# The second layer's up products by Strassen's scheme, over pairs of chunks

## The chip, the cores and the metric

The kernel runs on one core of one Trainium2 chip. The metric is the device time of one execution, in microseconds, as the median of several runs. Beside it there is one profiled execution, whose trace gives every instruction's start and duration on each engine: TensorE (PE, with its weight loads as PEld), VectorE (DVE), ScalarE (ACT), GpSimd (POOL) and SyncE (SP), which issues the transfers.

## What is computed

A gated linear recurrence over 4 sequences, 8 heads and 768 positions gives 3072 tokens of 256 numbers. Two layers of the same shape follow, each with an up product (256 to 2048), an activation and a down product (2048 to 256):

```python
x = attn_out.transpose(0, 2, 1, 3).reshape(3072, 256)
# first layer
h = x @ moe_w_in                                    # 256 x 2048
g = np.maximum(h, 0.0) + np.log1p(np.exp(-np.abs(h)))   # softplus
x = g @ moe_w_out                                   # 2048 x 256
# second layer
h = x @ moe2_w_in
g = np.where(h >= 1, h, np.where(h <= -1, 0.0, (h + 1) ** 2 / 4))
out = g @ moe2_w_out
```

## The kernel before

**Tiling.** The tokens are cut into six chunks `c` of 512 columns (`NC`, `T`). The hidden width is cut into 16 blocks `fc` of 128. A step `s` is one layer `m`, one chunk and one block (in the first two chunks of the first layer two blocks of 256 columns): 96 steps a layer. All products run on operands that are split into a high and a low part, so that each 128x128 block of weights by 512 columns takes three matmuls (high by high, low by high, high by low). A step's `up` (L902) has two row blocks k of the input, hence 6 matmuls into one PSUM bank; its `down` (L953) has two output halves e, again 6, which accumulate over the 16 blocks in two banks named acc. A step of the second layer is thus 12 matmuls.

**Between up and down.** In the first layer ScalarE computes softplus (`g`, L933). In the second, for the first 24 steps (`on_act`, `ACT_UNTIL` = 120) ScalarE does three activations (L917, L918, L925) and VectorE one instruction (L937). From then on ScalarE does one (L920) and VectorE two (L939, L940). `g_hi` casts the result to the high part, on ScalarE (L510) or VectorE (L512), and `g_lo` subtracts to get the low part (L948). Slots bound how far this runs ahead: 2 t, 3 g, 3 gh, 3 gl.

**Order.** Nothing is scheduled while it runs. `Jobs.order` (L46) is a list scheduler that runs when the program is built: each job has an engine (or several with a cost in ns each, of which it takes the one that ends first), needs, slots that it takes and gives back, and a due time. The job that can start earliest is placed next, ties on one engine go to the earlier due time. It fixes which engine does a job, the order on each engine and the buffers. Costs and latencies are constants in the code; `SHARED` lists by how much VectorE and GpSimd jobs lengthen each other. `mlp_steps` (L156) gives the order of the steps: the second layer begins with chunks 0 and 1 in two halves of the width, then takes chunks 2 to 5 one after another. The recurrence (`spread`, `decay`, `weigh`, `scores`, `out`, `ready`) runs between the first layer's steps, with due times from `CHUNK`.

**PSUM.** Eight banks: four acc, two h, and a pair that the recurrence uses until its last `ready`, after which it becomes two banks z. `up` takes h, or from step 16 on also z and acc when they are free.

**Weights.** They arrive as 64-bit floats and are turned into 32 bits by `w0` to `w3`, then split by `w_hi` and `split_w`. There is one set of split tiles `wt`, so a block of the second layer replaces that of the first after its last use. Before, up to 16 blocks of the second layer wait in tiles that the recurrence has left (`spare`, L531), and four staging tiles st take the loads.

**Ends of chunks.** `finish_hi` copies a chunk's two acc banks to SBUF (`finish_lo` adds the low part after the first layer), and `store` sends the output.

Of the kernel before, what the change touches and what calls it, by code (L numbers as in the profile page):

```python
# [15 lines left out]
Q = 128  # L16
# [139 lines left out]
def mlp_steps():  # L156

    steps = []
    for c, sub, fc, n_fc in ORDER:
        if sub is None:  # L160
            steps += [(0, c, 0, T, fc + i, 1) for i in range(n_fc)]
        else:
            steps += [(0, c, sub * 256, 256, fc + 2 * i, 2) for i in range(n_fc // 2)]
    done = {c for c, _, _, _ in ORDER}
    steps += [(0, c, 0, T, i, 1) for c in range(NC) if c not in done for i in range(NFC)]
    steps += [(1, c, 0, T, i + 8 * part, 1) for part in range(2) for c in range(2) for i in range(NFC // 2)]
    steps += [(1, c, 0, T, i, 1) for c in range(2, NC) for i in range(NFC)]
    return steps

# [11 lines left out]
def whole(s):  # L181

    return s < WHOLE
# [12 lines left out]
def program():  # L196
# [117 lines left out]
    for m in range(2):  # L314
        for j in sorted(range(8), key=lambda j: first_use[m, j]):
            for kind in "io":
                w = (m, kind, j)
                add(("load_w", *w), SP, 400, takes=["sx" if m == 0 and j == SX else "st"], size=524e3)
# [12 lines left out]
                add(("w_hi", *w), {ACT: 520, DVE: 350}, needs=[("w2" if signed(*w) else "w3", *w)] + ([last_use[0, kind, j]] if m else []))  # L331
                add(("split_w", *w), {DVE: 610, POOL: 1500}, needs=[("w_hi", *w)], gives=[("w0", *w)] * m)


    for s, (m, c, t0, n, fc, m_fc) in enumerate(steps):
# [8 lines left out]
        bank = ("h",) if s < H_MORE else ("h", "z") if 96 <= s < 128 else ("h", "z", "acc")  # L344
        add(("up", s), PE, up, due=when(s), needs=needs, takes=[bank])
# [8 lines left out]
        elif on_act(s):  # L354
            add(("act_first", s), ACT, 1050, needs=[("up", s)], takes=["t"])
            add(("act_last", s), ACT, 530, needs=[("act_first", s)])
            add(("g", s), DVE, 610, needs=[("act_last", s)], takes=["g"], gives=[("act_first", s), ("up", s)])
        else:
            add(("act_first", s), ACT, 500, needs=[("up", s)], takes=["t"])
            add(("g", s), DVE, 1260, needs=[("act_first", s)], takes=["g"], gives=[("act_first", s), ("up", s)])  # L360
# [3 lines left out]
        else:  # L364
# [6 lines left out]
            ("down", s), PE, down, due=when(s) + LAG, needs=needs,  # L371
            takes=["acc"] * ((1 if n == 256 else 2) * first), gives=gives,
        )
        if fc + m_fc == NFC:
            root = ("down", min(r for r in range(len(steps)) if steps[r][:3] == (m, c, t0)))
            for e in range(2):
                own = when(s) + LAG + 2000 if m else None
                add(("finish_hi", s, e), {ACT: 490 if n == T else 280, DVE: 610 if n == T else 340}, due=own, needs=[("down", s)],
                    takes=["osb"] * m, gives=[("part", root, e)] * m)
# [7 lines left out]
    slots = dict(sx=2, h=2, y=1, z=0, acc=4, t=2, g=N_G, gh=3, gl=3, ld=5, u=4, bc=3, bt=3, dec=2, st=4, w32=16, osb=4)  # L387
# [28 lines left out]
CHUNK = 16  # L416
# [7 lines left out]
LAG = 1500  # L424
DEC_DMAS = 1
# [9 lines left out]
def tile_kernel(ctx: ExitStack, tc: tile.TileContext, a0, al, bc, ub, w_in, w_out, w2_in, w2_out, out):  # L435
# [56 lines left out]
    for tag, dtype, n in (("xh", F32R, NC), ("xl", F32R, NC), ("ld", F32, 5), ("gh", F32R, 3), ("gl", F32R, 3), ("u", F32, 4), ("dec", F32, 2)):  # L492
# [3 lines left out]
    raw_t = [base.tile([128, 2, 256, 2], U32, name=f"st{i}") for i in range(4)]  # L496
    eye_t = base.tile([128, H * Q], F32, name="eye_t")
# [3 lines left out]

    xh, xl, xw = {}, {}, {}

# [27 lines left out]
    spare = [("ld", 0, 0), ("ld", 0, 1), ("ld", 1, 0), ("ld", 1, 1), ("ld", 2, 0), ("ld", 2, 1), ("ld", 3, 0), ("ld", 3, 1)]  # L531
    spare += [("ld", 4, 0), ("ld", 4, 1), ("bc", 2, 0), ("w32", 0, 0)] + [("u", i, 0) for i in range(4)]

    def raw(*w):
        tag, i = got["load_w", *w][0]
        if tag == "sx" and i not in raw_x:
# [4 lines left out]
    def w32(m, kind, j):  # L541
# [7 lines left out]
        else:  # L549
            tag, i, part = spare[got["w0", m, kind, j][0][1]]  # L550
            t = buf(tag, i)
            t = (flat(t) if tag == "ld" else t)[:, part * 512:part * 512 + 512]
# [53 lines left out]
    def w3(engine, *w):  # L606
# [3 lines left out]
        )  # L610

# [290 lines left out]
    def up(engine, s):  # L902
        m, c, t0, n, fc, m_fc = steps[s]
        ph = mine("up", s)[0]
        for j in range(m_fc):
# [22 lines left out]
    def g(engine, s):  # L928
        ph, g = mine("up", s)[0], mine("g", s)[0]
# [174 lines left out]
```

## Time and profile before

| | us |
|---|---|
| median of 3 runs | 589.9 (589.9 to 590.36) |
| span of the profiled execution | 588.6 |
| TensorE busy | 578.5 |
| VectorE busy | 469.5 |
| ScalarE busy | 256.8 |
| GpSimd busy | 17.5 |

The profile comes from one execution of its own, so its span stands a little beside the median. A matmul is shown with its whole passage through the array, which overlaps the next one; the distance between two starts is what it costs. A timeline row has the start and the duration in us, the engine, the line of the code, the operation, what it writes and reads by the names of the tiles, the shapes, and in brackets how long the engine stood idle before and what ended the wait.

### The profile page before, as it was taken

The numbers are of one execution on the slowest core, as the hardware profiler recorded it, in microseconds if no ns is written. First come the engines' busy times: TensorE is split into PE (matmuls) and PEld (weight loads), VectorE is DVE, ScalarE is ACT, GpSimd is POOL, SyncE is SP. The second block draws the span as 40 slices with busy tenths as digits, with TensorE's granted clock in tenths as the row PEclk, the third lists the DMA queues.
The fourth block names the chain that finished last, engine by engine and source line by source line (L and its number), as shares of the span: only waits on it lengthen the run. The fifth ranks groups of instructions, "written<-read, shape, count | busy, mean of one in ns | idle before, by whom it ended". The sixth has DMA issues, their size and how long they took to land.

```text
span 588.6 us, 9187 instructions
## 1 busy us (share of the span) xinstructions
PE 578.5 (98%) x3598; PEld 482.6 (82%) x3598; DVE 469.5 (80%) x779; ACT 256.8 (44%) x460; POOL 17.5 (3%) x27
## 2 busy tenths in 40 slices
PE   7799999999999999999999999999999999999997
PEld 3699999997787788778888888888888888888885
DVE  6899999955865774479997866679899899899895
ACT  5858443523432332246656867643222322322321
POOL 4210100000000000000000000000000000000000
PEclk9999999999999999999999999999999999999999
DMA  7977436402410210006320000000000000000000
GB/s 282 388 276 214 136 115 241 158 1 77 142 69 28 108 72 0 1 2 213 120 98 0 1 1 2 0 37 0 37 0 1 36 2 1 37 0 2 36 1 36
DMA packets 19862, 43.67 MB, mean 74 GB/s; under 512 B 1740, under 2 KB 2316, under 8 KB 19820
## 3 DMA queue, kind: packets, MB, share of 16 engines
q1 hardware_dynamic: 19820, 43.10, 21.3%
q8 instruction: 28, 0.46, 0.3%
q14 instruction: 14, 0.11, 0.1%
HBM read 39.75 MB, written 3.34 MB: 73 GB/s over the span
## 4 chain that ended last, share of the span: by engine, by line
PE 95%; DMA 3%; DVE 0%; SPq 0%; issue 0%; ACT 0%
PE acc L974 44%; PE h L909 11%; PE h L911 11%; PE h L910 11%; PE acc L909 2%; PE acc L910 2%; PE acc L911 2%; DMA bc<-in_bc_dram 2%; PE z L909 2%; PE z L911 2%; PE z L910 2%; PE acc L962 2%; PE y L800 2%; PE y L842 2%; DMA st<-in_w_out_dram 1%; PE y L835 1%
## 5 line engine op out<-in xcount | busy, mean ns | idle before, releaser
L974 PE MATMUL acc<-gh,woh 128*128 128x512 f32 (+1 forms) x424 | 151.8, 366 | 0.0
L974 PE MATMUL acc<-gh,wol 128*128 128x512 f32 (+1 forms) x424 | 150.6, 363 | 0.0
L948 DVE TENSOR_TENSOR gl<-g,gh 128x512 fp32r<-128x512 f32 x183 | 127.3, 697 | 18.3 <-ACT gh L510 7.1
L909 PE MATMUL h<-xh,wih 128*128 128x512 f32 (+1 forms) x332 | 119.8, 361 | 0.0
L911 PE MATMUL h<-xl,wih 128*128 128x512 f32 (+1 forms) x332 | 118.1, 356 | 0.0
L910 PE MATMUL h<-xh,wil 128*128 128x512 f32 (+1 forms) x332 | 118.1, 356 | 0.0
L974 PE MATMUL acc<-gl,woh 128*128 128x512 f32 (+1 forms) x424 | 115.4, 363 | 0.0
L512 DVE CAST gh<-g 128x512 fp32r<-128x512 f32 x118 | 50.4, 427 | 53.3 <-ACT g L933 45.1
L974 PEld LDWEIGHTS acc<-gh,woh 128*128 128x128 f32 x424 | 79.9, 188 | 14.1 <-issue 1.1
L974 PEld LDWEIGHTS acc<-gh,wol 128*128 128x128 f32 x424 | 80.0, 189 | 12.3
L920 ACT ACTIVATE t<-h 128x512 f32<-128x512 f32 x63 | 37.7, 599 | 112.0 <-PE h L911 112.0
L974 PEld LDWEIGHTS acc<-gl,woh 128*128 128x128 f32 x424 | 74.4, 189 | 12.6
L909 PEld LDWEIGHTS h<-xh,wih 128*128 128x128 f32 x332 | 62.7, 189 | 11.1 <-issue 2.0
L911 PEld LDWEIGHTS h<-xl,wih 128*128 128x128 f32 x332 | 62.7, 189 | 9.0
L933 ACT ACTIVATE g<-h 128x512 f32<-128x512 f32 x55 | 32.8, 597 | 85.2 <-PE h L911 77.6
L910 PEld LDWEIGHTS h<-xh,wil 128*128 128x128 f32 x332 | 62.7, 189 | 8.7
L939 DVE SCALAR_TENSOR_TENSOR t<-t 128x512 f32<-128x512 f32 x72 | 49.6, 689 | 6.4 <-ACT t L920 6.1
L510 ACT CAST gh<-g 128x512 fp32r<-128x512 f32 x68 | 42.2, 621 | 19.2 <-DVE g L940 16.8
L764 DVE TENSOR_TENSOR_SCAN ld<-ld,eye_t 128x1024 f32<-128x1024 f32 x20 | 45.6, 2282 | 0.0
L940 DVE TENSOR_TENSOR g<-h,t 128x512 f32<-128x512 f32 x63 | 43.6, 692 | 2.2
L933 ACT ACTIVATE g<-acc 128x512 f32<-128x512 f32 x28 | 16.8, 598 | 38.2 <-PE acc L911 38.2
L909 PE MATMUL acc<-xh,wih 128*128 128x512 f32 (+1 forms) x68 | 24.0, 354 | 0.0
(148 smaller groups left out, 627.6 us busy)
## 6 DMA issues: line engine op xcount, KB each, us to landing
ld<-clip_z SPq DMA_DIRECT2D x20, 512.0 KB, 7.9
st<-in_w_in_dram SPq DMA_DIRECT2D x15, 512.0 KB, 4.3
st<-in_w_out_dram SPq DMA_DIRECT2D x15, 512.0 KB, 3.4
u<-in_ub_dram SPq DMA_DIRECT2D x24, 256.0 KB, 4.7
bc<-in_bc_dram SPq DMA_DIRECT2D x12, 384.0 KB, 3.1
out_dram<-dec SPq DMA_DIRECT2D x6, 256.0 KB, 2.2
dec<-clip_p SPq DMA_DIRECT2D x5, 256.0 KB
out_dram<-bc SPq DMA_DIRECT2D x5, 256.0 KB
```

The costliest lines, as they stand in the source:

```text
L510: nc.scalar.copy(out, in_)
L512: engines[engine].tensor_copy(out, in_)
L764: nc.vector.tensor_tensor_scan(t, t, eye_t, 0.0, ALU.mult, ALU.add)
L909: nc.tensor.matmul(o, wh, xh[c][:, k, t0:t0 + n], start=(k == 0), stop=False)
L910: nc.tensor.matmul(o, wl, xh[c][:, k, t0:t0 + n], start=False, stop=False)
L911: nc.tensor.matmul(o, wh, xl[c][:, k, t0:t0 + n], start=False, stop=(k == 1))
L920: nc.scalar.activation(out=t, in_=ph, func=AF.Relu, bias=0.5, scale=0.5)
L933: nc.scalar.activation(out=g, in_=ph, func=AF.Softplus)
L939: nc.vector.scalar_tensor_tensor(out=t, in0=t, scalar=1.0, in1=t, op0=ALU.min, op1=ALU.mult)
L940: nc.vector.tensor_tensor(out=g, in0=ph, in1=t, op=ALU.max)
L948: engines[engine].tensor_tensor(out=mine("g_lo", s)[0], in0=mine("g", s)[0], in1=mine("g_hi", s)[0].bitcast(F32), op=ALU.subtract)
L974: nc.tensor.matmul(acc_t(s, e), w, g[:, j * n:(j + 1) * n], start=(begins(e, j) and g is gh and i == 0), stop=(fc + j == NFC - 1 and g is ...
```

## The change

**The scheme.** For two chunks and a block of 256 by 256 weights (two rows k by two blocks fc) the four results C are 2x2 block products. Instead of 8 block products of three matmuls the new code makes 7, with the Winograd form of Strassen's scheme. Three sums of weight blocks (S) are made per 256 columns of weights (`s_sum`, four subtractions or additions of 128x128 on VectorE or GpSimd, then `s_hi` and `s_lo` split them). Four sums T of the input are made per pair of chunks (`t_sum`: eight instructions of 128x512 on GpSimd, `t_hi` on GpSimd or ScalarE, `t_lo` on GpSimd or VectorE); one of them goes into the place of an input that is not used any more.

**A quad** is the four steps of two blocks and two chunks. TensorE makes two products into two banks (`p15`); ScalarE copies the first bank into a third (`fork`) and the second into SBUF (`keep`); TensorE adds a product to the first bank, which is then result 0, and one to the third (`p26`); VectorE writes third bank plus kept tile into a fourth bank (`add1`); TensorE adds a product to the third and one to the fourth, which is then result 1 (`p37`); VectorE adds the kept tile and the third bank in SBUF, result 3 (`add2`); TensorE adds the last product to the third bank, result 2 (`p4`). The activations read these results. `p15` of a quad also needs `add1` of the one before.

**Order and places.** Chunks 4 and 5 of the first layer alternate step by step, and the second layer goes through the pairs (0,1), (2,3), (4,5) with all 16 blocks each. First-layer ups take h and z banks only, a quad takes all four of h and z. Downs of the second layer fall due 18 us after their step instead of 1.5 (`LAG_2`). There are 4 gh, 3 staging tiles for the second layer's loads instead of 4, 3 tiles w32 for its work instead of 16, and 2 cs; the freed tiles hold the S and T parts, and outputs leave through w32 or cs. `CHUNK` goes from 16 to 14.

```diff
-    steps += [(0, c, 0, T, i, 1) for c in range(NC) if c not in done for i in range(NFC)]
-    steps += [(1, c, 0, T, i + 8 * part, 1) for part in range(2) for c in range(2) for i in range(NFC // 2)]
-    steps += [(1, c, 0, T, i, 1) for c in range(2, NC) for i in range(NFC)]
+    steps += [(0, c, 0, T, i, 1) for c in range(NC - 2) if c not in done for i in range(NFC)]
+    pairs = [(0, NC // 2 - 1)] + [(1, p) for p in range(NC // 2)]
+    steps += [(m, c, 0, T, i, 1) for m, p in pairs for i in range(NFC) for c in (2 * p, 2 * p + 1)]
...
-        return up, (8 * m_fc * n / 2.4 if whole(s) else up)
+        return (up * 7 / 8 if m else up), (8 * m_fc * n / 2.4 if whole(s) else up)
...
+                w_made = ("s_sum", j) if m and kind == "i" else ("w2" if signed(*w) else "w3", *w)
+                add(("w_hi", *w), {ACT: 520, DVE: 350}, needs=[w_made] + ([last_use[0, kind, j]] if m else []))
...
+                    add(("s_sum", j), {DVE: 800, POOL: 1900}, needs=[("w3", *w)], takes=[("cs", "w32")])
+                    add(("s_hi", j), {ACT: 420, DVE: 280}, needs=[("s_sum", j)])
+                    add(("s_lo", j), {DVE: 470, POOL: 1200}, needs=[("s_hi", j)], gives=[("s_sum", j)])
...
+        late = [[("ready", NU - 1)], [("w3", 1, kind, 7) for kind in "io"] + [("p4", first + 3)], [("p4", first + 9)]][p]
+        t = [("t_sum", p, i) for i in range(4)]
+        add(t[0], POOL, 4100, needs=done + late, takes=[("cs", "w32")] * 3)
+        add(t[2], POOL, 1400, needs=[t[0]])
+        add(t[1], POOL, 1400, needs=[t[2]])
+        add(t[3], POOL, 2800, needs=[t[1], ("t_lo", p, 2)])
+        for i in range(4):
+            add(("t_hi", p, i), {POOL: 700, ACT: 520}, needs=[t[i]])
+            add(
+                ("t_lo", p, i), {POOL: 1500, DVE: 610}, needs=[("t_hi", p, i)] + [("t_lo", p, k) for k in (0, 1, 2) if i == 3],
+                gives=[t[0]] * (i == 3),
+            )
...
-        bank = ("h",) if s < H_MORE else ("h", "z") if 96 <= s < 128 else ("h", "z", "acc")
-        add(("up", s), PE, up, due=when(s), needs=needs, takes=[bank])
+        bank = ("h",) if s < H_MORE else ("h", "z")
...
+                needs += [("split_w", 1, "i", j), ("s_lo", j)] + [("t_lo", p, i) for i in range(4)]
+                needs += [("add1", q - 1)] * (s > NFC * NC)
+                add(("p15", q), PE, 2 * one, due=when(s), needs=needs, takes=[bank, bank])
+                add(("fork", q), ACT, 500, due=when(s) + 2300, needs=[("p15", q)], takes=[bank])
+                add(("keep", q), ACT, 500, due=when(s) + 2900, needs=[("fork", q)], takes=["cs"], gives=[("part", ("p15", q), 1)])
+                add(("p26", q), PE, 2 * one, due=when(s) + 2700, needs=[("fork", q)])
+                add(("add1", q), DVE, 610, due=when(s) + 5000, needs=[("p26", q), ("keep", q)], takes=[bank])
+                add(("p37", q), PE, 2 * one, due=when(s) + 5400, needs=[("add1", q)])
+                add(("add2", q), DVE, 610, due=when(s) + 7700, needs=[("p37", q)])
+                add(("p4", q), PE, one, due=when(s) + 8100, needs=[("add2", q)])
...
-            ("down", s), PE, down, due=when(s) + LAG, needs=needs,
+            ("down", s), PE, down, due=when(s) + (LAG_2 if m else LAG), needs=needs,
...
-    slots = dict(sx=2, h=2, y=1, z=0, acc=4, t=2, g=N_G, gh=3, gl=3, ld=5, u=4, bc=3, bt=3, dec=2, st=4, w32=16, osb=4)
+    slots = dict(sx=2, h=2, y=1, z=0, acc=4, t=2, g=N_G, gh=4, gl=3, ld=5, u=4, bc=3, bt=3, dec=2, st=3, st3=1, w32=3, cs=2)
...
-CHUNK = 16
+CHUNK = 14
...
+LAG_2 = 18000
...
+    @job
+    def t_sum(engine, p, i):
...
+        if i == 0:
+            total(a, c + 1, 0)
+            total(b, c, 0)
+            less(b, a, b)
+            total(d, c + 1, 1)
+        elif i == 2:
+            less(a, d, a)
+        elif i == 1:
+            less(d, d, b)
+        else:
+            total(a, c, 1)
+            less(a, a, d)
...
+    def product(bank, w, x, start):
+
+        (wh, wl), (bh, bl) = w, x
+        nc.tensor.matmul(bank, wh, bh, start=start, stop=False, skip_group_check=True)
+        nc.tensor.matmul(bank, wl, bh, start=False, stop=False, skip_group_check=True)
+        nc.tensor.matmul(bank, wh, bl, start=False, stop=True, skip_group_check=True)
...
+    @job
+    def fork(engine, q):
+        seeded(("fork", q))
+        nc.scalar.copy(mine("fork", q)[0], mine("p15", q)[0])
...
+    @job
+    def add1(engine, q):
+        seeded(("add1", q))
+        nc.vector.tensor_tensor(out=mine("add1", q)[0], in0=mine("fork", q)[0], in1=cs(q), op=ALU.add)
```

## Rows read from the trace of the kernel before

**Rows 1.** The page, busy time and share of the span by engine

```profile
PE 578.5 (98%) x3598; PEld 482.6 (82%) x3598; DVE 469.5 (80%) x779; ACT 256.8 (44%) x460; POOL 17.5 (3%) x27
```

**Rows 2.** Windows of 20 us: busy us by engine, TensorE's clock, DMA share, GB/s

```profile
160.00:180.00 20.00, 20.00 (x90) 16.55 (x89) 11.88 (x17) 7.36 (x15) 0.00 (x0) 1.00 0.22 77
...
280.00:300.00 20.00, 20.00 (x90) 16.54 (x90) 18.40 (x35) 13.09 (x23) 0.00 (x0) 1.00 0.37 126
...
480.00:500.00 20.00, 20.00 (x90) 16.57 (x89) 18.18 (x31) 4.20 (x7) 0.00 (x0) 1.00 0.00 0
```

**Rows 3.** Timeline, second layer: start us, us, engine, line, operation [idle before <-releaser]

```profile
479.96 0.39 PE L909 MATMUL h<-xh,wih 128*128 128x512 f32 x1
...
481.10 0.39 PE L911 MATMUL h<-xl,wih 128*128 128x512 f32 x1
...
481.52 0.60 ACT L920 ACTIVATE t<-h 128x512 f32<-128x512 f32 x1 [2.12 <-PE h L911]
...
482.16 0.69 DVE L939 SCALAR_TENSOR_TENSOR t<-t 128x512 f32<-128x512 f32 x1
...
490.85 0.39 PE L909 MATMUL h<-xh,wih 128*128 128x512 f32 x1
```

**Rows 4.** Timeline of VectorE alone, just behind a change of chunk in the second layer

```profile
427.27 0.69 DVE L940 TENSOR_TENSOR g<-h,t 128x512 f32<-128x512 f32 x1
428.07 0.43 DVE L512 CAST gh<-g 128x512 fp32r<-128x512 f32 x1
428.60 0.69 DVE L948 TENSOR_TENSOR gl<-g,gh 128x512 fp32r<-128x512 f32 x1
429.21 0.69 DVE L939 SCALAR_TENSOR_TENSOR t<-t 128x512 f32<-128x512 f32 x1
429.93 0.69 DVE L940 TENSOR_TENSOR g<-h,t 128x512 f32<-128x512 f32 x1
```

**Rows 5.** Timeline of VectorE, instructions without dependence on each other, first layer

```profile
239.48 0.68 DVE L809 TENSOR_TENSOR ld<-y,ld 128x512 f32<-128x512 f32 x1
240.08 0.68 DVE L809 TENSOR_TENSOR ld<-acc,ld 128x512 f32<-128x512 f32 x1
```

**Rows 6.** Groups by form: count | busy us, mean ns | idle before, releaser

```profile
L948 DVE TENSOR_TENSOR gl<-g,gh 128x512 fp32r<-128x512 f32 x183 | 127.3, 697 | 18.3 <-ACT gh L510 7.1
...
L510 ACT COPY dec<-acc 128x512 f32<-128x512 f32 x5 | 2.7, 589 | 4.3 <-PE acc L974 4.3
...
L510 ACT CAST gh<-g 128x512 fp32r<-128x512 f32 x68 | 42.2, 621 | 19.2 <-DVE g L940 16.8 <-PE acc L974 0.8
...
L933 ACT ACTIVATE g<-acc 128x512 f32<-128x512 f32 x28 | 16.8, 598 | 38.2 <-PE acc L911 38.2
```

**Rows 7.** Timeline of VectorE where ScalarE does the activation

```profile
348.81 0.69 DVE L948 TENSOR_TENSOR gl<-g,gh 128x512 fp32r<-128x512 f32 x1
350.20 0.69 DVE L937 SCALAR_TENSOR_TENSOR g<-h,t 128x512 f32<-128x512 f32 x1 [0.70 <-ACT t L925]
```

**Rows 8.** Timelines of GpSimd and of VectorE in the same stretch

```profile
59.15 1.31 POOL L948 TENSOR_TENSOR gl<-g,gh 128x512 fp32r<-128x512 f32 x1 [6.23 <-ACT w L576]
...
59.65 1.35 DVE L948 TENSOR_TENSOR gl<-g,gh 128x512 fp32r<-128x512 f32 x1 [0.36 <-ACT gh L510]
...
64.68 0.68 DVE L809 TENSOR_TENSOR ld<-acc,ld 128x512 f32<-128x512 f32 x1
...
64.87 1.30 POOL L948 TENSOR_TENSOR gl<-g,gh 128x512 fp32r<-128x512 f32 x1 [4.42 <-DVE wol L618]
...
65.28 1.44 DVE L948 TENSOR_TENSOR gl<-g,gh 128x512 fp32r<-128x512 f32 x1
```

**Rows 9.** Timeline of the end

```profile
579.02 0.39 PE L911 MATMUL h<-xl,wih 128*128 128x512 f32 x1
...
582.13 0.69 DVE L948 TENSOR_TENSOR gl<-g,gh 128x512 fp32r<-128x512 f32 x1
...
584.46 0.39 PE L974 MATMUL acc<-gl,woh 128*128 128x512 f32 x1
```

More of the change, by code (lines that the diff above doesn't have):

```diff
@@ L317, in program @@
                 w = (m, kind, j)
-                add(("load_w", *w), SP, 400, takes=["sx" if m == 0 and j == SX else "st"], size=524e3)
+                add(("load_w", *w), SP, 400, takes=["sx" if m == 0 and j == SX else "st" if m else ("st", "st3")], size=524e3)
                 add(
@@ L342, in program @@
         up, down = pe_time(s)
-        bank = ("h",) if s < H_MORE else ("h", "z") if 96 <= s < 128 else ("h", "z", "acc")
-        add(("up", s), PE, up, due=when(s), needs=needs, takes=[bank])
+        bank = ("h",) if s < H_MORE else ("h", "z")
+        made, frees = ("up", s), ("up", s)
+        if m == 0:
+            add(("up", s), PE, up, due=when(s), needs=needs, takes=[bank])
+        else:
+            q, role = quad_of(s), s % 4
+            made = [("p26", q), ("p37", q), ("p4", q), ("add2", q)][role]
+            frees = [("part", ("p15", q), 0), ("add1", q), ("fork", q), ("keep", q)][role]
+            if role == 0:
+                j, p = fc // 2, c // 2
+                one = up * 8 / 7 / 2
+                needs = [("finish_lo", 0, i, t, e) for i in (c, c + 1) for t in tokens[i] for e in range(2)]
+                needs += [("split_w", 1, "i", j), ("s_lo", j)] + [("t_lo", p, i) for i in range(4)]
[8 more added lines that the diff above has]
+                add(("p4", q), PE, one, due=when(s) + 8100, needs=[("add2", q)])
         before = [("down", r) for r in range(s) if steps[r][:3] == (m, c, t0)][-1:]
@@ L549, in w32 @@
         else:
[L550 to L552 removed]
+            t = plain(*spare[got["w0", m, kind, j][0][1]])
         return t.rearrange("p (k f) -> p k f", k=2)
@@ L904, in up @@
         ph = mine("up", s)[0]
+        (whole_banks.add if n == T else whole_banks.discard)(got["up", s][0])
         for j in range(m_fc):
@@ new lines, in seeded, with p15, keep @@
+    def seeded(name):
+        assert got[name][0] in whole_banks, name
+    @job
+    def p15(engine, q):
+        w, s, x, t, c = operands(q)
+        whole_banks.update(got["p15", q])
+        a, d = mine("p15", q)
+        product(a, w(0, 0), x(c, 0), True)
+        product(d, s(0), t(0), True)
+    @job
+    def fork(engine, q):
+        seeded(("fork", q))
+        nc.scalar.copy(mine("fork", q)[0], mine("p15", q)[0])
+    @job
+    def keep(engine, q):
+        nc.scalar.copy(cs(q), mine("p15", q)[1])
@@ new lines, in p26, with p37 @@
+    @job
+    def p26(engine, q):
+        w, s, x, t, c = operands(q)
+        product(mine("p15", q)[0], w(1, 0), x(c, 1), False)
+        product(mine("fork", q)[0], s(1), t(1), False)
+    @job
+    def add1(engine, q):
+        seeded(("add1", q))
+        nc.vector.tensor_tensor(out=mine("add1", q)[0], in0=mine("fork", q)[0], in1=cs(q), op=ALU.add)
+    @job
+    def p37(engine, q):
+        w, s, x, t, c = operands(q)
+        product(mine("add1", q)[0], s(3), x(c + 1, 1), False)
+        product(mine("fork", q)[0], s(2), t(2), False)
@@ new lines, in add2, with cs, p4, made_of @@
+    @job
+    def add2(engine, q):
+        nc.vector.tensor_tensor(out=cs(q), in0=mine("fork", q)[0], in1=cs(q), op=ALU.add)
+    def cs(q):
+        return temp("keep", q)[0]
+    @job
+    def p4(engine, q):
+        w, s, x, t, c = operands(q)
+        product(mine("fork", q)[0], w(1, 1), t(3), False)
+    def made_of(s):
+        q = quad_of(s)
+        if q is None:
+            return mine("up", s)[0]
+        return [lambda: mine("p15", q)[0], lambda: mine("add1", q)[0], lambda: mine("fork", q)[0], lambda: cs(q)][s % 4]()
```

104 lines of the change are left out of this document (89 added, 15 removed).

## The prediction

> **What bounds the kernel now.** I read first the page's busy table and then the windows: TensorE is busy for 20.00 us of every 20 us in the first layer, in the preparation of the second layer's weights and in the second layer alike, always at clock 1.00 [rows 1, 2]. So the bound is TensorE's own instruction stream. VectorE, at 18.18 of 20, is close behind it in the second layer and far from it in the first (11.88) [rows 2].
>
> Next the timeline of one stretch of the second layer. Between 479.96 and 490.85 four steps pass, that is 48 matmuls in 10.89 us: 2.72 us a step, 0.227 us a matmul [rows 3]. (A matmul's 0.39 us overlaps its neighbour; only the distance between starts counts.) The same rows give the price of a round trip through another engine. The last up matmul starts at 481.10, its slot is over at 481.33, ScalarE runs from 481.52 to 482.12, and VectorE starts on the result at 482.16: 0.83 us in which TensorE needs other work [rows 3].
>
> Then VectorE by itself, where it is catching up and nothing but itself sets its pace: from one max (L940) to the next 2.66 us [rows 4]. In it the second activation instruction follows the first after 0.72. Instructions that don't wait for each other follow each other every 0.60 us, although each is shown with 0.68 [rows 5]; without the cast of L512 the step would thus be 0.72 + 0.60 + 0.60 = 1.92 us, and a cast that stands between a max and its subtraction costs VectorE 0.74. These are the prices below. The page's 0.697 for a subtraction [rows 6] would overstate VectorE's load.
>
> **What is removed.** Two weight blocks by two chunks make a quad: four steps of the old order. It needed 8 block products of 3 matmuls and now needs 7. Per quad 24 + 24 matmuls become 21 + 24: 45 x 0.227 = 10.21 us instead of 10.89. There are 24 quads, so 72 matmuls or 16.3 us go, all from the engine that is the bound. The number of matmuls is fixed by the code, so this part can't fail; the question is only what TensorE waits for.
>
> **What is added inside a quad.** Up products no longer run in any order. p26 waits for a ScalarE copy from PSUM to PSUM (fork), p37 for VectorE's add1, p4 for add2. TensorE is in order: behind a waiting product stand the down matmuls that were planned after it, and they can't pass. No row shows an engine writing PSUM. The nearest for fork and keep is the PSUM copy of 0.589 us [rows 6]; for the adds it is L809, one PSUM and one SBUF operand, 0.60 apart [rows 5]. From below I bound an add by the 0.43 of a cast [rows 4], from above by 0.60 plus the 1.32 of a two-instruction activation that stands ahead of it on VectorE. I take 0.60, since the shapes are those of L809.
>
> One down between two products is 6 x 0.227 = 1.36 us, which covers a trip of 0.83. Four gaps, four downs: a quad can be dense. The four free banks bind little: the bank that fork fills is the last to come free, after p4, the activation and VectorE, some 0.83 + 1.32 us plus what is queued, and the next add1 comes two downs and two products after p4, 4 x 1.36 us.
>
> VectorE per quad, without casts: four times 0.72 + 0.60 + 0.60, and two adds of 0.60: 8.88 us against TensorE's 10.21. That leaves room for 1.8 casts at 0.74. ScalarE has four activations at 0.60, fork and keep at 0.59 and up to four casts at 0.62: 6.1 us [rows 3, 6]. In the first six quads, where ScalarE does the activation, VectorE still waits 0.70 us per step [rows 7], so the adds fit. I take an average stall of 0.1 us a quad, 2.4 us in all, between 0 and 8 (0.33 a quad).
>
> **What is added around the quads.** (1) Filling. Before, the first second-layer ups needed nothing from each other. Now the first quad has three trips and only the last downs of the first layer to put between them, and its own first down comes after an activation on ScalarE, a cast and a subtraction. I count three uncovered trips, 3 x 0.83 = 2.5 us (0 to 5).
>
> (2) Two changes of pair. All four acc banks are now one pair's. After the even chunk's last down two copies of 0.59 each free its banks, behind the odd chunk's last down of 1.36 and the next pair's products. I take 0.6 us each, 1.2 us in all (0 to 2.8).
>
> (3) The sums of the chunks (T) on GpSimd: eight 128x512 instructions a pair, 1.31 us each by the nearest row [rows 8]. GpSimd has nothing else then, so nobody queues behind their waits for finish_lo and p4; but they run beside VectorE. When GpSimd ran such an instruction from 59.15, VectorE's subtraction took 1.35 us instead of 0.69, and again 1.44 at 65.28; L809, with one operand in PSUM, took its usual 0.68 [rows 4, 5, 8]. A collision costs 0.66 to 0.75, eight cost 5.6 us. The Trainium skill's page "SBUF — State Buffer", section "Who interferes with whom", says that a VectorE instruction with two SBUF inputs and a GpSimd instruction that reads SBUF exclude each other, the loser blocked for the other's whole instruction; the trace agrees, for the subtraction of 59.65 ends 0.54 us after GpSimd's 60.46. By that rule's worst case the eight would cost the whole GpSimd time, 10.5 us instead of 5.6.
>
> For the first pair all this falls into the first layer, for the second into the quads with a waiting VectorE. The third pair's T meets the full VectorE. With one cast a quad it has 10.21 - 9.62 = 0.6 us to spare, 1.1 in two quads, and one finished down in store is worth 1.36: 5.6 - 1.1 - 1.4 = 3.1 us are left (0 to 10.5). The planner's SHARED table has no entry for these jobs, so its order makes no allowance. The four t_lo of a pair on VectorE and t_hi on ScalarE are in the slack of the quads around.
>
> (4) The tail. Before, the last up starts at 579.02, the last subtraction at 582.13, and queued downs cover it until 584.46 [rows 9]. Now the last quad leaves, after p37, 0.83 + 0.60 + 3 x 1.92 = 7.2 us of trip, add2 and VectorE steps, against p4 and four downs, 0.68 + 5.4 = 6.1 us: 1.1 us (0 to 4).
>
> **What moves at no cost.** The weights of the second layer go through 3 staging and 3 work tiles instead of 4 and 16, and each block adds s_sum, s_hi and s_lo, at most six VectorE instructions. Before, this work filled VectorE to 18.40 of 20 while TensorE stayed full [rows 2]. Now chunks 4 and 5 free block j every four steps and it is wanted again 28 steps (76 us) later, so it spreads over twice the time; uncovered, it would be 8 x 6 x 0.60 = 29 us of VectorE. The loads wait longer on SP, where only later weight loads stand behind them. Attention falls due up to ten steps earlier; VectorE was busy for 11.88 of 20 there [rows 2]. The first layer's ups lose the acc banks, in which 28 of them ran [rows 6]. Two h banks alternate with a down of 1.36 between, longer than the trip; if that cover fails I see at most 3 us.
>
> **The sum.** 588.6 - 16.3 + 2.4 + 2.5 + 1.2 + 3.1 + 1.1 = 582.6 us of span. The median of the runs shown, 589.9, is 1.3 above the profiled span, so the forecast is 583.9 us. About 0.2% (1.2 us) is what a measurement can tell from no change here.
>
> **The rivals.**
> - VectorE becomes the bound (slower). Place: the 18 quads from the second part of pair 0 on, where VectorE does the activation. The planner puts a cast on whichever engine ends it first, and lists 360 ns for VectorE and 520 for ScalarE. With h casts a quad VectorE needs 8.88 + 0.74 h: it binds from h = 1.8, and the gain is gone at 2.4. With three, 11.1 us, the 18 quads lose 16.4 us, in place of 1.8 of the 2.4 above: 597.2 + 1.3 = 598.5. For it: before, the casts stood on VectorE in this stretch [rows 4]. Against it: they did when VectorE had nothing else ready right after the max; with adds and other steps' work waiting, ScalarE ends them earlier. 0.18.
> - The trips stay uncovered (no change). A two-instruction activation ahead of add1 makes the trip 0.83 + 1.32, longer than one down. A stall of 0.35 us per quad instead of 0.1 eats the rest: 589.9. For it: VectorE is 87% full without casts. Against it: ups run ahead of downs by several steps, so a second down is usually there. 0.14.
> - Everything is hidden. The terms (1) to (4) and the stalls come to between 0 and 5 us: 573.6 to 579. For it: TensorE shows no gap before, through a layer change, too. Against it: filling and collisions have no cover that I can name. 0.17.
> - The forecast, 579 to 588.6: 0.48. Something worse in the first layer or the weights: 0.03.
>
> **How the numbers follow.** Faster by over 0.2%: 0.48 + 0.17 and the lower edge of the second rival, 0.03: 0.68. Within: 0.11. Slower: 0.21. For 8 in 10 the range leaves out the very best of the hidden case and the worst third of the VectorE case: 575 to 596.
>
> **What would show it.** Right: the matmuls of the second layer's up lines number 504 instead of 576, and the gaps on TensorE sit at the start of the second layer, in quads 10 to 13, and at the end. A stretch of a late quad without GpSimd takes 10.2 to 10.3 us, with at most two casts on VectorE. Wrong: VectorE gapless at 10.6 us or more a quad (first rival), TensorE waiting for add1 or add2 in every quad while VectorE has gaps (second), idle TensorE before 330 us (weights or banks), or subtractions beside GpSimd that last 0.69.

## The result: slower, by a term that was five times too small

The median is 596.44 us (593.02 to 596.8) against 590.13 us for the kernel before on the same chip: a ratio of 1.0093, 95% interval 1.0065 to 1.0121. The forecast was 583.9 us, so the sign was wrong, and the time lies 0.4 us beyond the upper end of the range. The profiled execution spans 595.1 us, 6.5 more than before.

From the page after come the busy times, as in [rows 1], and the chain of work that ended last, by engine:

```profile
PE 571.3 (96%) x3526; PEld 471.6 (79%) x3526; DVE 504.5 (85%) x814; ACT 322.1 (54%) x584; POOL 68.4 (11%) x60
...
PE 82%; DVE 12%; issue 2%; DMA 2%; ACT 2%; SPq 0%; DVEq 0%; ACTq 0%
```

Before, that chain was almost all TensorE's:

```profile
PE 95%; DMA 3%; DVE 0%; SPq 0%; issue 0%; ACT 0%
```

The 72 matmuls are gone, 3526 instead of 3598, and TensorE is busy for 7 us less. But VectorE now has 12% of the chain.

The windows say where (columns as in [rows 2]); the first line is the hole's place in the kernel before, the others are the kernel after:

```profile
420.00:440.00 20.00, 20.00 (x90) 16.57 (x89) 18.10 (x31) 4.79 (x8) 0.00 (x0) 1.00 0.01 1
...
320.00:340.00 20.00, 17.99 (x77) 13.89 (x76) 14.37 (x25) 16.42 (x28) 0.00 (x0) 1.00 0.00 0
360.00:380.00 20.00, 18.22 (x81) 14.75 (x80) 17.43 (x26) 16.92 (x31) 7.09 (x5) 1.00 0.00 1
420.00:440.00 20.00, 14.86 (x53) 11.45 (x52) 18.07 (x23) 8.22 (x16) 8.03 (x6) 0.83 0.00 1
440.00:460.00 20.00, 17.96 (x71) 13.86 (x70) 19.41 (x25) 8.71 (x16) 9.77 (x6) 0.91 0.00 0
500.00:520.00 20.00, 18.50 (x80) 14.37 (x79) 15.00 (x26) 8.61 (x15) 0.00 (x0) 1.00 0.14 53
540.00:560.00 20.00, 20.00 (x90) 16.57 (x89) 19.24 (x32) 11.04 (x21) 0.00 (x0) 1.00 0.00 0
```

From 460 on TensorE is as full as before, but for 1.5 us at 500 to 520, where pair 2 begins. The other losses are 2.0 us at 320 to 340, some 2 to 3 at 350 to 380, and a hole at 420 to 460: there 7.2 us are missing from busy TensorE, and its granted clock is 0.83 and 0.91 on the mean of a window. VectorE is busy for 18.07 and 19.41 of 20 us in the hole, and GpSimd works 8.03 and 9.77 us of 20, where it did nothing before.

TensorE's own timeline in the hole:

```profile
422.27 0.39 PE L1194 MATMUL acc<-gh,wol 128*128 128x512 f32 x1
425.50 0.73 PE L1194 MATMUL acc<-gl,woh 128*128 128x512 f32 x2 [2.85 <-DVE gl L1168]
428.52 0.80 PE L1064 MATMUL h<-xh,ld_later 128*128 128x512 f32 x1 [2.29 <-DVE h L1107]
429.12 0.63 PE L1065 MATMUL h<-xh,ld_later 128*128 128x512 f32 x1
429.54 0.63 PE L1066 MATMUL h<-xl,ld_later 128*128 128x512 f32 x1
...
435.06 0.39 PE L1066 MATMUL z<-xl,ld_later 128*128 128x512 f32 x1
435.29 0.40 PE L1064 MATMUL h<-st_later,wih 128*128 128x512 f32 x1
```

Two waits of 2.85 and 2.29 us lie close to each other, the first for a subtraction, the second for add1 (L1107). Behind them two matmuls are 0.42 us apart (429.12 to 429.54) and take 0.63; from 434 on it is 0.23 and 0.39 again. That is the lower of the clock's two levels, 1.2 GHz instead of 2.4.

VectorE in the same stretch, as in [rows 4], and then GpSimd, as in [rows 8]:

```profile
418.96 1.71 DVE L1159 SCALAR_TENSOR_TENSOR t<-t 128x512 f32<-128x512 f32 x1
420.71 1.66 DVE L1160 TENSOR_TENSOR g<-more_plain,t 128x512 f32<-128x512 f32 x1
422.40 1.38 DVE L609 CAST gh<-g 128x512 fp32r<-128x512 f32 x1
423.70 1.75 DVE L1168 TENSOR_TENSOR gl<-g,gh 128x512 fp32r<-128x512 f32 x1
425.37 1.76 DVE L1159 SCALAR_TENSOR_TENSOR t<-t 128x512 f32<-128x512 f32 x1
427.17 0.69 DVE L1160 TENSOR_TENSOR g<-z,t 128x512 f32<-128x512 f32 x1
427.78 0.69 DVE L1107 TENSOR_TENSOR h<-h,more_plain 128x512 f32<-128x512 f32 x1
```

```profile
418.83 1.30 POOL L729 TENSOR_TENSOR dec_plain<-xh,xl 128x512 f32<-128x512 f32 x1 [41.59 <-DMA out_dram<-dec_plain]
420.08 1.74 POOL L729 TENSOR_TENSOR st_plain<-xh,xl 128x512 f32<-128x512 f32 x1
421.90 1.60 POOL L732 TENSOR_TENSOR st_plain<-dec_plain,st_plain 128x512 f32<-128x512 f32 x1
423.46 1.44 POOL L729 TENSOR_TENSOR st_plain<-xh,xl 128x512 f32<-128x512 f32 x1
424.98 1.60 POOL L732 TENSOR_TENSOR dec_plain<-st_plain,dec_plain 128x512 f32<-128x512 f32 x1
426.66 1.60 POOL L732 TENSOR_TENSOR st_plain<-st_plain 128x512 f32<-128x512 f32 x1
...
440.46 1.73 POOL L757 TENSOR_TENSOR u_later<-dec_plain,u_later 128x512 fp32r<-128x512 f32 x1 [12.20 <-ACT u_later L607]
...
445.50 1.75 POOL L757 TENSOR_TENSOR xl<-st_plain,xh 128x512 fp32r<-128x512 f32 x1
447.20 1.75 POOL L757 TENSOR_TENSOR u_later<-st_plain,u_later 128x512 fp32r<-128x512 f32 x1
448.92 1.46 POOL L757 TENSOR_TENSOR eye_later<-dec_plain,eye_later 128x512 fp32r<-128x512 f32 x1
```

Five VectorE instructions in a row, which took 0.69 or 0.43 in [rows 4], take 1.38 to 1.76. Each ends just behind a GpSimd instruction: the cast 0.28 us behind, the four others, which have two operands in SBUF, 0.55 (418.96 + 1.71 against 418.83 + 1.30 and so on). The max at 427.17, which reads PSUM, and the add1 at 427.78 keep their 0.69, although GpSimd works from 426.66 to 428.26. The max at 420.71 is the same instruction of line L1160, but its operand is the quad's fourth result, which lies in SBUF (more_plain): 1.66. GpSimd is not left alone either, its instructions take 1.30 to 1.75. The four lines of L757 are of the second burst: pair 2's four t_lo (u_later, xl, eye_later) run on GpSimd as well, where the prediction had them on VectorE.

From here on idle time is read off TensorE's timeline by the distance between starts, which gives 0.16 us more than the brackets, since a matmul's 0.39 us reach into the gap behind it. There are 5.5 us idle and 2.6 us lost to half clock at 422 to 434, 2.4 and 1.7 at 451 to 458, together 12 us. Two waits beside pair 1's sums, at 358 to 364, come to 2.6 us.

### The profile page after: what moved, and what is told of

It reads as the page before. It is cut to its first block, busy times and chain, and to the rows that moved or that the text cites. A ratio compares the mean times of both kernels' runs of the same rounds, so it can differ in the third digit from the quotient of the medians.

```text
span 595.1 us, 9154 instructions
## 1 busy us (share of the span) xinstructions
PE 571.3 (96%) x3526; PEld 471.6 (79%) x3526; DVE 504.5 (85%) x814; ACT 322.1 (54%) x584; POOL 68.4 (11%) x60
## 4 chain that ended last, share of the span: by engine, by line
PE 82%; DVE 12%; issue 2%; DMA 2%; ACT 2%; SPq 0%; DVEq 0%; ACTq 0%
PE acc L1194 37%; PE h L1057 6%; PE h L1059 6%; PE h L1058 6%; PE h L1064 3%; PE h L1066 3%; PE h L1065 3%; PE z L1064 3%; PE z L1066 2%; PE z L1065 2%; DVE gl L1168 2%; DVE t L1159 2%; PE y L947 2%; DMA bc<-in_bc_dram 2%; PE acc L1182 2%
## 5 line engine op out<-in xcount | busy, mean ns | idle before, releaser
L607 ACT CAST gh<-g 128x512 fp32r<-128x512 f32 x131 | 81.4, 621 | 43.4 <-DVE g L1160 24.6
L1194 PEld LDWEIGHTS acc<-gh,woh 128*128 128x128 f32 x424 | 80.4, 190 | 16.1 <-issue 1.7
L1057 PE MATMUL h<-xh,wih 128*128 128x256 f32 (+1 forms) x224 | 74.9, 334 | 0.0
L1058 PE MATMUL h<-xh,wil 128*128 128x256 f32 (+1 forms) x224 | 73.6, 328 | 0.0
L1059 PE MATMUL h<-xl,wih 128*128 128x256 f32 (+1 forms) x224 | 73.6, 328 | 0.0
L609 DVE CAST gh<-g 128x512 fp32r<-128x512 f32 x55 | 27.7, 508 | 22.9 <-ACT g L1153 22.4
L1057 PEld LDWEIGHTS h<-xh,wih 128*128 128x128 f32 x224 | 42.5, 190 | 4.7 <-issue 0.7
L1059 PEld LDWEIGHTS h<-xl,wih 128*128 128x128 f32 x224 | 42.5, 190 | 3.9
L1058 PEld LDWEIGHTS h<-xh,wil 128*128 128x128 f32 x224 | 42.6, 190 | 3.7
L1140 ACT ACTIVATE t<-h 128x512 f32<-128x512 f32 x27 | 16.2, 600 | 11.9 <-PE h L1066 11.6
L1160 DVE TENSOR_TENSOR g<-h,t 128x512 f32<-128x512 f32 x27 | 18.7, 692 | 0.9
```

The costliest lines, as they stand in the source:

```text
L607: nc.scalar.copy(out, in_)
L1057: nc.tensor.matmul(o, wh, xh[c][:, k, t0:t0 + n], start=(k == 0), stop=False)
L1058: nc.tensor.matmul(o, wl, xh[c][:, k, t0:t0 + n], start=False, stop=False)
L1059: nc.tensor.matmul(o, wh, xl[c][:, k, t0:t0 + n], start=False, stop=(k == 1))
L1140: nc.scalar.activation(out=t, in_=ph, func=AF.Relu, bias=0.5, scale=0.5)
L1194: nc.tensor.matmul(acc_t(s, e), w, g[:, j * n:(j + 1) * n], start=(begins(e, j) and g is gh and i == 0), stop=(fc + j == NFC - 1 and g is ...
```

## The experiments

Two theories stand against each other. Either GpSimd's sums T hold VectorE up, and TensorE through it. Or the scheme itself does it: the waits inside the quads, a VectorE that is full anyway, the new order.

**Sums for the first pair only.**

```diff
-    for p in range(NC // 2):
+    for p in range(1):
...
-                needs += [("split_w", 1, "i", j), ("s_lo", j)] + [("t_lo", p, i) for i in range(4)]
+                needs += [("split_w", 1, "i", j), ("s_lo", j)] + [("t_lo", 0, i) for i in range(4)]
...
-        t = lambda i: [t_of(p, i, lo) for lo in range(2)]
+        t = lambda i: [t_of(0, i, lo) for lo in range(2)]
```

> The kernel after, but the sums T are made for the first pair only; the quads of pairs 1 and 2 multiply with pair 0's sums, so that their results are not the reference's. Everything else stays. Theory (GpSimd's sums hold up VectorE, and TensorE with it): in the kernel after TensorE lost 2.6 us at 355 to 364 and 12.6 us at 420 to 458 (7.9 idle, 4.7 at half clock), both beside GpSimd's sums; without them 596.4 - 15.2 = 581.2, between 579 and 584, and no window of the second layer with a clock under 1.00. Rival (the waits inside the quads, or a VectorE that is too full by itself): the idle stretch at 420 to 458 stays, and only the sums' few instructions on VectorE and ScalarE go: 592 to 596.

Measured: 580.1 us (580.02 to 581.72), ratio 0.9822 (0.9794 to 0.9849). Its windows:

```profile
320.00:340.00 20.00, 17.94 (x77) 13.91 (x76) 14.36 (x25) 15.83 (x27) 0.00 (x0) 1.00 0.00 0
420.00:440.00 20.00, 19.33 (x86) 15.69 (x85) 19.22 (x32) 11.48 (x20) 0.00 (x0) 1.00 0.01 1
440.00:460.00 20.00, 20.00 (x90) 16.57 (x89) 19.20 (x32) 10.88 (x19) 0.00 (x0) 1.00 0.00 0
```

The hole is gone and the clock is 1.00; the start of the second layer and 0.8 us at each change of pair remain. So products in lockstep, fork, keep, add1 and add2 are nearly free: everything else in the change, taken together, is worth 10 us, and the sums of pairs 1 and 2 cost 16.3 us (596.44 less 580.10). What this kernel cannot tell is whether it is the collision or the mere work of the sums that costs.

**The same sums on VectorE.** t_sum is cut into eight jobs of one instruction each; pairs 1 and 2 have them and t_lo on VectorE.

```diff
-        add(t[0], POOL, 4100, needs=done + late, takes=[("cs", "w32")] * 3)
...
+        on, cost = (DVE, 610) if p in T_DVE else (POOL, 1400)
...
-                ("t_lo", p, i), {POOL: 1500, DVE: 610}, needs=[("t_hi", p, i)] + [("t_lo", p, k) for k in (0, 1, 2) if i == 3],
+                ("t_lo", p, i), {DVE: 610} if p in T_DVE else {POOL: 1500, DVE: 610}, needs=[("t_hi", p, i)] + [("t_lo", p, k) for k in (0, 1, 2) if i == 3],
...
+T_DVE = (1, 2)
```

> The kernel after with all sums T of pairs 1 and 2 on VectorE, as single instructions (8 sums, 4 low parts a pair); pair 0's stay on GpSimd. Theory (the collision is the cost, not the work): an instruction on VectorE costs it 0.60 us, one on GpSimd beside it 1.07; 7.2 us a pair, spread by the planner, against about 4 us of slack in eight quads: 581 to 588, clock 1.00 throughout the second layer. Rival (VectorE has no room for the sums wherever they run): 7.2 us a pair come out as TensorE's idle time, 592 to 597.

Measured: 584.76 us (583.81 to 587.15), ratio 0.9898 (0.9857 to 0.9939): faster than the kernel before, with all the work done. Windows, and three lines of VectorE's timeline, the middle one a sum:

```profile
420.00:440.00 20.00, 19.37 (x86) 15.70 (x85) 19.50 (x33) 11.53 (x21) 0.00 (x0) 1.00 0.00 1
440.00:460.00 20.00, 20.00 (x90) 16.57 (x89) 18.89 (x31) 10.69 (x20) 0.00 (x0) 1.00 0.00 0
```

```profile
371.61 0.68 DVE L1165 TENSOR_TENSOR gl<-g,gh 128x512 fp32r<-128x512 f32 x1
372.20 0.68 DVE L736 TENSOR_TENSOR dec_plain<-st_plain,dec_plain 128x512 f32<-128x512 f32 x1
372.81 0.68 DVE L1165 TENSOR_TENSOR gl<-g,gh 128x512 fp32r<-128x512 f32 x1
```

The sum's neighbours start 0.60 us before and after it. VectorE has more to do than in the kernel after, 833 instructions instead of 814, and TensorE waits less. So it is the collision, not the work: an engine that helps a full VectorE from the side took more of its time than the work itself is. One more thing differs, since eight single jobs let the planner spread the sums; what spreading does on GpSimd is seen below.

**The collision by itself, first try.** Into the kernel before go 12 additions on GpSimd whose result nobody reads, one behind the other or spread.

```diff
+    for k in range(12):
+        add(("idle_sum", k), POOL, 1400, needs=[("up", 136 + 0 * k)] + [("idle_sum", k - 1)] * (k > 0))
...
+    @job
+    def idle_sum(engine, k):
+        nc.gpsimd.tensor_tensor(out=scratch, in0=xh[5][:, 0].bitcast(F32), in1=xl[5][:, 0].bitcast(F32), op=ALU.add)
```

> The kernel before plus 12 additions of 128x512 on GpSimd, one behind the other from step 136 on (second layer, VectorE at 2.66 of 2.72 us a step), into a tile that nobody reads. Theory (a VectorE instruction with two SBUF inputs, or a cast, waits for a whole GpSimd instruction): 12 x 1.07 = 12.8 us for VectorE, almost all of it idle TensorE, with half clock after the longest gaps: 601 to 607. By the price in the prediction, 0.70 each: 598. Rival (the gaps after have another cause, GpSimd only happened to run then): 590.

> As the run with the burst, but each of the 12 additions waits for two more steps, so that one comes every 5.4 us. Theory: the same collisions, one at a time, 12 x 1.07 us less 24 x 0.06 of slack = 11.4 us, in pieces of about 1 us, clock 1.00: 600 to 602, some 4 us under the burst, which is what the clock costs there. If VectorE can catch up between two of them: 592 to 596.

Measured: 591.99 and 592.81 us, against 590.09 for the kernel before. Each is a single run, and the kernel before reached 592.66 in one of its seven. Both missed their stretch: a need in the planner's list is no wait on the chip unless the job reads what the other wrote. The additions read only chunk 5, and so they ran as one burst as soon as that was ready, in both kernels (the first one's line; in the other from 328.86 for 18.71 us):

```profile
328.03 18.72 POOL L947 TENSOR_TENSOR scratch<-xh,xl 128x512 f32<-128x512 f32 x12 [262.66 <-DVE xl L1005]
```

There ScalarE still does the activation. What VectorE's timeline shows beside the burst:

```profile
339.43 1.60 DVE L955 TENSOR_TENSOR gl<-g,gh 128x512 fp32r<-128x512 f32 x1
340.95 0.68 DVE L940 SCALAR_TENSOR_TENSOR g<-z,t 128x512 f32<-128x512 f32 x1
341.73 0.73 DVE L515 CAST gh<-g 128x512 fp32r<-128x512 f32 x1
```

The subtraction takes 1.60 instead of 0.69 and the cast 0.73 instead of 0.43, but the max, which reads PSUM, keeps its 0.68, and VectorE's slack of 0.70 us per step [rows 7] takes most of it: the distances between TensorE's starts add up to 2.2 us more than before at 320 to 360, in both kernels. So a collision is cheaper where VectorE has time to spare.

**The collision by itself, second try.** Now an addition reads the result g of step 136, or of steps 136, 138 and so on, and thereby waits for it. The burst, against the kernel before:

```diff
+    for k in range(12):
+        add(("idle_sum", k), POOL, 1400, needs=[("g", 136 + 0 * k)] + [("idle_sum", k - 1)] * (k > 0))
...
+        nc.gpsimd.tensor_tensor(
+            out=scratch, in0=mine("g", 136 + 0 * k)[0] if 0 or k == 0 else xh[5][:, 0].bitcast(F32), in1=xl[5][:, 0].bitcast(F32), op=ALU.add
+        )
```

and spread, where each addition reads its own g:

```diff
+    for k in range(12):
+        add(("idle_sum", k), POOL, 1400, needs=[("g", 136 + 2 * k)] + [("idle_sum", k - 1)] * (k > 0))
...
+        nc.gpsimd.tensor_tensor(
+            out=scratch, in0=mine("g", 136 + 2 * k)[0] if 2 or k == 0 else xh[5][:, 0].bitcast(F32), in1=xl[5][:, 0].bitcast(F32), op=ALU.add
+        )
```

> The kernel before plus 12 additions of 128x512 on GpSimd into a tile that nobody reads. The first reads step 136's result, so that this time the burst falls where VectorE does the activation (in the two runs with additions so far it ran at 328 to 347, beside ScalarE's activation, and cost 2 us). There a GpSimd instruction took 1.56 us and let one VectorE instruction with two SBUF inputs pass. Theory: a step has three that must pass (the first activation instruction, the cast, the subtraction), so it takes 4.7 us while GpSimd runs; 18.7 us pass 4 steps instead of 6.9, 7.9 us idle, and 2 to 5 us of half clock behind it: 598 to 604. Rival (GpSimd beside VectorE costs little, the gaps after have another cause): 590 to 593.

> As the burst at step 136, but each of the 12 additions reads the result of two steps later than the one before, so that one comes every 5.4 us. Theory: the same collisions one at a time, up to 1.05 us each less 0.12 of slack in two steps: 597 to 601, in gaps of 1 us and less, clock 1.00 throughout; the difference to the burst is then the clock. If one at a time finds cover: 590 to 593.

Measured: 598.42 us for the burst, 598.34 us spread, a single run of each, against 590.02 (589.65 to 592.26 in 18 runs) for the kernel before. VectorE's timeline in the burst:

```profile
436.42 1.77 DVE L942 SCALAR_TENSOR_TENSOR t<-t 128x512 f32<-128x512 f32 x1
438.23 0.69 DVE L943 TENSOR_TENSOR g<-h,t 128x512 f32<-128x512 f32 x1
439.02 0.58 DVE L515 CAST gh<-g 128x512 fp32r<-128x512 f32 x1
439.71 1.59 DVE L957 TENSOR_TENSOR gl<-g,gh 128x512 fp32r<-128x512 f32 x1
441.23 1.77 DVE L942 SCALAR_TENSOR_TENSOR t<-t 128x512 f32<-128x512 f32 x1
```

A step goes from one first activation instruction to the next in 4.81 us (436.42 to 441.23) instead of the 2.66 of [rows 4], while about three additions pass, one every 1.56 us. Two instructions of the step are held up by about 1 us each, the cast by 0.15. A window of the burst, then one of the spread additions:

```profile
440.00:460.00 20.00, 16.45 (x62) 12.14 (x61) 18.72 (x22) 2.99 (x5) 11.46 (x8) 0.91 0.00 0
```

```profile
480.00:500.00 20.00, 16.97 (x72) 13.07 (x71) 18.31 (x26) 3.72 (x7) 4.60 (x3) 1.00 0.00 1
```

In the burst TensorE's granted clock is 0.91 on the window's mean; spread, it stays at 1.00 and of its nine gaps one is 2.15 us, the others 0.3 to 0.7. The burst costs 8.4 us and the spread additions 8.3, that is 0.70 us for each addition; spreading brings nothing. I had expected the 2 to 5 us of half clock as the difference between them. That was wrong: the burst has waits of 1.30, 1.85 and 1.92 us and some 1.7 us of half clock behind them, the spread additions have 6.9 us of waits. What a GpSimd instruction costs a kernel with a full VectorE is thus measured without any of the change's other parts.

**ScalarE's activation in the quads of pair 2's sums.**

```diff
-    return NFC * NC <= s < ACT_UNTIL
+    return NFC * NC <= s < ACT_UNTIL or 128 <= s < 152
```

> The kernel after, but ScalarE does the activation also in steps 128 to 151 (quads 8 to 13), where GpSimd makes pair 2's sums; the sums stay on GpSimd. Theory (collisions hurt where VectorE has no time to spare): VectorE gets 0.72 us a step back and has one instruction less that can collide; the 12.6 us at 420 to 458 shrink to 2 to 5: 586 to 589, clock 1.00. Rival (GpSimd's sums come too late by themselves, so that TensorE waits for them): no change, 594 to 597; or ScalarE becomes the bound in these quads: over 597.

Measured: 589.29 us (587.95 to 589.95), ratio 0.9982 (0.9973 to 0.9992), 0.3 us above the stretch that was expected. The window of the first burst:

```profile
420.00:440.00 20.00, 17.59 (x68) 13.59 (x69) 18.20 (x25) 14.61 (x27) 9.52 (x7) 0.91 0.00 1
```

In this window GpSimd is as busy as in the kernel after, but TensorE is idle for 2.4 us instead of 5.1, and the clock is 0.91 instead of 0.83. Slack on VectorE shortens the hole and does not close it. But not all of the 7.1 us against the kernel after are its work: with the new load the planner also put pair 2's four t_lo on VectorE (L757 at 438 to 446), so that eight instructions instead of 12 run on GpSimd. The kernel to compare with is the next one, at 591.72 us, and ScalarE's activation is worth 2.4 us.

**t_lo on VectorE.**

```diff
-                ("t_lo", p, i), {POOL: 1500, DVE: 610}, needs=[("t_hi", p, i)] + [("t_lo", p, k) for k in (0, 1, 2) if i == 3],
+                ("t_lo", p, i), {DVE: 610} if p else {POOL: 1500, DVE: 610}, needs=[("t_hi", p, i)] + [("t_lo", p, k) for k in (0, 1, 2) if i == 3],
```

> The kernel after, but the four low parts t_lo of pairs 1 and 2 are on VectorE alone, as the prediction had assumed; the planner had put pair 2's four on GpSimd. Theory: the second burst (440 to 450 in the kernel after) loses four of its six instructions, the first keeps its six; of the 12.6 us the 4.3 at 450 to 458 go, and the four cost VectorE 2.4: 591 to 593.

Measured: 591.72 us (590.2 to 592.03), ratio 1.0016 (1.0002 to 1.0029):

```profile
420.00:440.00 20.00, 15.37 (x59) 11.77 (x59) 19.15 (x24) 9.34 (x17) 8.52 (x6) 0.83 0.01 1
440.00:460.00 20.00, 20.00 (x90) 16.57 (x89) 18.18 (x31) 10.68 (x19) 0.00 (x0) 1.00 0.00 0
```

The second hole is gone, the first is as good as unchanged. The four instructions that I had placed on the wrong engine were worth 4.7 us. Beside pair 1's sums, at 360 to 380, the clock is 0.91 here and was 1.00 in the kernel after, with the same two waits of 0.67 and 1.94 us: the same waits took the clock down in one profiled execution and not in the other.

**The order alone.** The kernel before with the new `mlp_steps`, CHUNK 14, and ups in h and z banks only.

```diff
+    pairs = [(0, NC // 2 - 1)] + [(1, p) for p in range(NC // 2)]
+    steps += [(m, c, 0, T, i, 1) for m, p in pairs for i in range(NFC) for c in (2 * p, 2 * p + 1)]
...
-        bank = ("h",) if s < H_MORE else ("h", "z") if 96 <= s < 128 else ("h", "z", "acc")
+        bank = ("h",) if s < H_MORE else ("h", "z")
...
-CHUNK = 16
+CHUNK = 14
```

> The kernel before with the order alone: chunks 4 and 5 of the first layer alternate, the second layer goes by pairs, ups take h and z banks only, CHUNK is 14; eight products, no sums. Theory (the loss sits in the sums on GpSimd, the order costs next to nothing): in the traces so far the first layer lost 1 to 2 us against the kernel before, and a change of pair 0 to 1 us: 590 to 593. Rival (the new order and the fewer banks cost by themselves what the quads were thought to lose): over 595.

Measured: 591.99 us (591.15 to 593.34), ratio 1.0023 (1.0006 to 1.0041). At the layer change TensorE is full but for 0.2 us:

```profile
320.00:340.00 20.00, 20.00 (x89) 16.31 (x88) 14.69 (x25) 15.95 (x27) 0.00 (x0) 1.00 0.00 1
```

So the order costs some 1.9 us. The profiled execution, the slowest of the ten with 593.34 us, shows 2.2 us of its loss in the first layer: 1.1 in the first 17 us, where kernels that differ only in the second layer lie as far apart (the same early matmul starts at 16.76 in the kernel after and at 15.58 in the run with ScalarE's activation), and most of the rest in one wait of 1.2 us for VectorE at 76 us. The losses at the start of the second layer belong to the quads.

**Can the remaining gaps be filled?** The kernel with the sums on VectorE, with later due times for the last downs of the first layer; then with CHUNK back at 16 as well.

```diff
-            ("down", s), PE, down, due=when(s) + (LAG_2 if m else LAG), needs=needs,
+            ("down", s), PE, down, due=when(s) + (LAG_2 if m else 9000 if s >= 90 else LAG), needs=needs,
```

```diff
-CHUNK = 14
+CHUNK = 16
```

> The kernel with the sums of pairs 1 and 2 on VectorE (584.8), and the downs of the first layer's last six steps due 9 us after their step instead of 1.5, so that they lie between the first quad's products. Theory (the three gaps at the start of the second layer, 0.95, 0.6 and 0.95 us, are trips with nothing to cover them): they close, 2.5 us less: 581.5 to 583.5. Rival (those downs are only moved, and the accumulators or the inputs come late for it): 584 to 587.

> As the run before it with CHUNK back at 16, so that the recurrence of the late chunks falls due up to eight steps later. If the earlier due times cost the first layer its 1 to 2 us: 580 to 582. If chunk 5, which is now wanted 15 steps earlier, comes late: over 585.

Measured: 584.57 us (583.74 to 585.07) and 584.44 us (584.31 to 584.98), not to be told from 584.76. The start of the second layer in the first of them:

```profile
320.00:340.00 20.00, 17.96 (x77) 13.88 (x76) 14.99 (x27) 16.26 (x28) 0.00 (x0) 1.00 0.00 0
```

The gaps of 0.95, 0.60 and 0.96 us are where they were: the downs moved, but not to the places where TensorE waits. For CHUNK neither of the two expected stretches came, and it is worth nothing that can be measured. All three kernels beat the one before by about 1%.

## Why the prediction was wrong, step by step

- *What is removed*, 16.3 us: right. 0.227 us a matmul still holds where nothing disturbs.
- *Inside a quad*, 2.4 us: nothing at all. TensorE has 20.00 of 20 in the undisturbed windows. The first rival (casts make VectorE the bound) falls: from 520 to 580 ScalarE does 21 of the casts and VectorE 3, half a cast per quad. Its price with three casts adds up to 18 x (11.10 - 10.21) = 16.0 us, not 16.4, which changes nothing. The second rival (uncovered trips) falls too: in those windows a down is always there.
- *(1) Filling*, 2.5 us: three gaps of 0.95, 0.61 and 0.94 us, as counted.
- *(2) Changes of pair*, 1.2 us: 0.8 at each one in the kernel without sums, 1.8 at the one that stands clear of the sums in the kernel after. The mechanism was another: TensorE waits for the add1 of the new pair's first quads, not for the banks.
- *(4) Tail*, 1.1 us: none. The last down starts at 590.72, 4.4 us before the end, against 4.1 before.
- *At no cost* was to be the first layer, with at most 3 us for its banks: the order, the banks and CHUNK together cost 1.9 us.
- *(3) The sums*, 3.1 us, is the term that failed: they cost about 15 us, 12 for pair 2 (some 1 us of it the first change of pair, which falls into the same stretch) and 2.6 for pair 1; without them the kernel is 16.3 us faster. The price of a collision came out: 0.70 us per GpSimd instruction in the prediction, 0.70 in the additions. That is in part luck. The prediction took one VectorE instruction, longer by 0.66 to 0.75; in the burst two of a step's four are longer by about 1 us while three GpSimd instructions pass, and 1.7 of the 8.4 us are half clock. What the price was multiplied with and set against was wrong. First, pair 2 had 12 instructions on GpSimd and not eight: 2.8 us more. The code leaves t_lo to the planner, which took GpSimd for the four; I set them down as VectorE's without bounding that. Second, I let 1.1 us of slack and 1.4 us of a finished down absorb part of it. Neither did: idle TensorE alone is 7.9 us, close to 12 x 0.70. Third, pair 1 was not hidden by the quads with a waiting VectorE; its sums cost 2.6 us there, and even the additions cost 2.2. Fourth, gaps of this length took the clock down, some 4.3 us, which stood in no term. 3.1 + 2.8 + 2.5 + 2.6 + 4.3 makes 15.3.

The Trainium skill's rule on the shared port ("SBUF — State Buffer", section "Who interferes with whom") says which instructions meet: a GpSimd instruction that reads SBUF holds up those of VectorE with two SBUF inputs, and VectorE's modes that use both ports, which a cast can enter, meet it too; other instructions with at most one SBUF input do not. The trace of the kernel after agrees, instruction by instruction: with two SBUF operands 1.66 to 1.76 us instead of 0.69, a cast 1.38 instead of 0.43, with an operand in PSUM 0.69 as ever. I had read the rule as an upper end, the whole GpSimd time of eight instructions or 10.5 us; the sums cost more, with 12 instructions on GpSimd for pair 2, pair 1's, and the clock.

The sum closes when all distances between TensorE's starts are counted against a stream with 0.227 us between two. The second layer of the kernel after then loses 21.5 us: 3.0 at 320 to 340, 3.5 at 340 to 400, 12.7 at 420 to 460 and 2.4 at 500 to 520. Less the 16.3 removed, that is 5.2 of the 6.5 us between the spans; 1.2 lie in the first layer, most of them in its first 17 us. By the same count the kernel without the sums loses 5.4 us, so that the sums cost 16.1. With the sums moved to VectorE the change gives 584.8 us, near the 583.9 that was forecast for it as it stood, but this is luck in part: it loses 9.1 us against the forecast's 10.3, with nothing inside the quads and in the tail, and more at the changes of pair.

## What to carry to other kernels

Before work goes to GpSimd to spare VectorE, look at how full VectorE is and at its operands: here two SBUF inputs or a cast waited until the GpSimd instruction was over, and on a full VectorE 0.60 us of its own work cost 0.70 as help from GpSimd, with the planner's four more instructions and the clock on top. Where a planner may choose an engine, a prediction needs both choices priced, and idle gaps on TensorE need a second term for the slower matmuls behind them. Strassen's scheme itself, with sums made by the engines between the products, can run with a full TensorE as long as enough other products are ready to stand in the gaps.

## What the runs showed of the hardware

- TensorE's granted clock fell to its lower level in the kernel after during the second of two waits of 3.01 and 2.46 us with two matmuls between, and again behind 1.00 and 1.37 us in the second burst; in the burst of additions it fell behind waits of 1.30, 1.85 and 1.92 us. It did not fall behind a single wait of 2.15 us, nor behind those of 0.3 to 0.7, in the spread ones; behind 0.67 and 1.94 us it fell in one kernel (t_lo on VectorE) and not in another (the kernel after). At half clock matmuls started 0.43 us apart instead of 0.227.
- A collision lengthens both sides: GpSimd's instruction went from 1.30 us up to 1.75, VectorE's from 0.69 up to 1.79. VectorE's ended 0.55 us behind the GpSimd instruction beside which it ran, a cast 0.28.
- One and the same VectorE instruction (L1160) took 0.69 us with an operand in PSUM and 1.66 with both in SBUF, beside the same GpSimd work.
